# A down projection's last product, divided once more into seven products of 256 columns

## The chip, the cores and the metric

The kernel runs on one core of one Trainium2 chip. The metric is the device time of one execution in microseconds. Before the change it is 525.81 us, the median of three runs (525.75 to 525.83). The core has five engines with a queue each: TensorE (PE in the profile, its weight loads PEld), VectorE (DVE), ScalarE (ACT), GpSimd (POOL) and SyncE (SP), which here issues the DMA transfers. Each engine works through its own queue in order, and semaphores order the queues against each other.

## The reference

```python
# x [1, 2048, 1024], w_gate and w_up [1024, 3584], w_down [3584, 1024], all bfloat16
g = jnp.einsum("bsd,df->bsf", x, w_gate)
u = jnp.einsum("bsd,df->bsf", x, w_up)
h = gelu_tanh(g) * u
return jnp.einsum("bsf,fd->bsd", h, w_down)
```

It is a gated feed-forward layer: two projections up, a product of one with the gelu of the other, and one projection down.

## The kernel before

The 2048 tokens are worked on as four groups of 512. Two groups at a time form a pass, and each pass has a down projection of its own: `down(0, ...)` for the first 1024 tokens and `down(1, ...)` for the rest, one after the other, at the end of the kernel. The change touches these two calls only. What comes before them, the projections up and the gelu, fills the first 346 us of the profile and writes h to DRAM (`hd`), from where it is loaded again in tiles `h[kh][c]`: `kh` is the half of the 3584 features (14 blocks of 128 each, `NJ = 14`), `c` is the group of 512 tokens.

**Seven products instead of eight.** A down projection is a product of 2x2 blocks: token groups by feature halves, times feature halves by output halves (512 columns each). It is made with seven block products and sums before and after them (the Strassen-Winograd form). A block product runs over 14 feature blocks, and for each of these over four banks of 128 tokens, so it has 56 matmuls of 128x128 weights by 512 columns. Four PSUM banks `e` and four banks `c` take the results. In order:

1. `e = h[0][0] * b11` in bf16, copied to `c`; then `c += h[1][0] * b21` in bf16, stored.
2. `e += s2 * t2` (copied out as `u2`), and three blocks behind it `c = s1 * t1` (copied out as `p5`).
3. `e += s3 * t3`, stored with `p5` added, and three blocks behind it `c += s4 * b22`, stored with `u2` added.
4. The last product, `e += h[1][1] * t4`, stored from `e` by ScalarE.

The sums `s1` to `s4` are of h and are made by VectorE (`make12`, `make73`), with results in fp32r, the 32-bit form that TensorE takes at one pass. `t1`, `t2` and `t4` are sums of w_down; they were made in earlier passes and lie in DRAM (`td`), from where `load12` and `load4` fetch them. `t3` is made by VectorE, and `b22` and h[1][1] are cast to fp32r by ScalarE (`tb`, `sa`).

**The second projection's last product is divided.** `down(1)` doesn't run step 4 as 56 matmuls of 512 columns. `inner_product` treats it as a 2x2 product again: 256 tokens (`r` counts its two groups of 128), 7 feature blocks (`H = 7`), 256 columns (`Q = 256`). It has seven products of 2 x 7 = 14 matmuls of 256 columns, 98 in all. `inner_sums` makes its sums s1 to s4 of h[1][1] on VectorE as four instructions of 1792 elements, two at step 20 and two at step 44. `inner_t`, `inner_t3` and `inner_t4` make t1 to t4 of the loaded t4 tiles (`q4`) on POOL, 28 differences of 128x256 elements. `inner_cast` casts the blocks of h[1][1] that are used as they are. z1, z6, z7 and z5 go to the four banks `c`, the other three products are added onto `e`, and VectorE adds both when it stores (`put`). `down(0)` doesn't do this: its step 4 is the plain one.

**What sets the order.** Every engine's order is written out by hand (`tc.manual_schedule`). A projection counts steps: `step(n)` is called before each chunk of 4 or 8 matmuls, from -1 to 75, and runs what `agenda` and `tails` hold for that step (`at`, `at_tail`), then `more(n)`, which for the first projection issues loads for the second. Steps 0 to 13 are the first half of product 1, 14 to 27 its second half, 28 to 44 stage 2, 45 to 61 stage 3, 62 to 75 the last product. ScalarE is ordered by the framework.

**Slots.** Most tiles come from one pool of 58 slots of 2 KB per partition (`slot`). A new tile takes the slot that comes free, and its first writer, a DMA or an engine, waits for the last readers of the tile that had it. DMA transfers all go out of SP's queue, eight semaphore lanes in turn: a transfer that isn't due yet holds up all those behind it.

**The turn from one projection to the next.** The loads of h for `down(1)` are issued by `more_0` in `down(0)`: h[0][0] at step 56, h[1][0] at 59, h[0][1] at 61 and h[1][1] at 63, the last one after the casts of step 4. The second projection's banks `e` are the first one's banks `c` and the other way round. With `SEAM = 3` the first projection holds its first three chunks back, and the first two banks of four chunks are then written before the other two; the second projection doesn't hold them at its start.

Of the kernel before, what the change touches and what calls it, by code (L numbers as in the profile page):

```python
# [10 lines left out]
def kernel(  # L11
# [29 lines left out]
    NJ = NFB // 2  # L41
    N = 512
# [9 lines left out]
    H, Q, R2 = NJ // 2, N // 2, range(2)  # L52
    SLOTS = 58
    STAGED = 3
    SEAM = 3
    LAG = 3
    BIG12 = (0,), (8, 10)
    AT12 = [0, 0, 1, 2, 4, 5, 9, 12, 16, 18, 22, 27, 29, 31], [4, 4, 8, 8, 12, 12, 15, 16, 18, 20, 22, 27, 29, 31]
    AT12S = [6, 7, 9, 10, 13, 14, 16, 18, 20, 23, 25, 27, 29, 31]
    EARLY = 8  # L60
    AT73 = [31 + 2 * j if j < 7 else 38 + j for j in range(NJ)]

    ctx.enter_context(tc.manual_schedule(engines=ORDER))
    xpool = ctx.enter_context(tc.tile_pool(name="x", bufs=1))
    hpool = ctx.enter_context(tc.tile_pool(name="h", bufs=1))
    wpool = ctx.enter_context(tc.tile_pool(name="w", bufs=2))
# [12 lines left out]
    def slot(shape, dtype, name):  # L79
        return kpool.tile(shape, dtype, name=name, tag="k")  # L80
# [18 lines left out]
    def new_h(kh, c):  # L99
        h[kh][c] = hpool.tile([P, NJ, N], bf16, name=f"h{kh}{c}")  # L100
# [4 lines left out]
    def dve(out, a, b, op):  # L105
        nc.vector.tensor_tensor(out=out, in0=a, in1=b, op=op)  # L106
# [4 lines left out]
    def new(eng, a, b, op, name, shape=None, dtype=None):  # L111
        t = slot(shape or [P, N], dtype or f32r, name)
        eng(t, a, b, op)
        return t

    def cast(src, name, shape=None):
        t = slot(shape or [P, N], f32r, name)
        nc.scalar.copy(out=t, in_=src)  # L118
        return t
# [386 lines left out]
    q12, s12, q73, q4, raw = {}, {}, {}, {}, {}  # L506
# [38 lines left out]
        tb = cast(rr[:, 1, :], "tb")  # L545
        q73[j] = s3, t3, s4, tb

    def make_sa(j):
        sa[j] = cast(h[1][1][:, j, :], "sa")

    def fetch12(n):
        kh, j = n // 7, 2 * (n % 7)
        if (1, n) in raw:
# [10 lines left out]
            raw[1, n] = big[:, n - n0]  # L564
            nc.sync.dma_start(out=raw[1, n], in_=wdn[:, kh, j : j + 2, :N])

    def inner_sums(late):
        hi = h[1][1][:, :H], h[1][1][:, H:]
        a11, a21 = hi[0][:, :, :Q], hi[0][:, :, Q:]
        a12, a22 = hi[1][:, :, :Q], hi[1][:, :, Q:]  # L570
        if not late:
            s1, s2 = [xpool.tile([P, H, Q], f32r, name=f"xT{n}") for n in range(2)]
            dve(s1, a21, a22, ADD)
            dve(s2, s1, a11, SUB)
            return s1, s2
        s3, s4 = [wpool.tile([P, H, Q], f32r, name="w") for _ in range(2)]
        dve(s3, a11, a21, SUB)
        dve(s4, a12, inner[1], SUB)
        return s3, s4

    def inner_t(t):
        b1, b2 = q4[t], q4[H + t]
# [27 lines left out]
    for j in range(NJ):  # L610
        at(AT12S[j], make12, j)
        at(AT73[j] - 4, fetch73, j)
        at(AT73[j], make73, j)
    sa, it, inner = {}, {}, []
    tails = {}, {}

    def at_tail(last, step, what, j):
        tails[last].setdefault(int(step), []).append((what, j))
# [3 lines left out]
    for j in range(NJ):  # L622
        for last in range(2):
            if last or j not in STAY:
                at_tail(last, AT12[last][j], lambda j, last=last: load12(j, BIG12[last]), j)
        at_tail(0, 49 + 0.65 * j, load4, j)
        at_tail(0, 54 + 0.55 * j, make_sa, j)
    for t in range(H):
        for j in (t, H + t):
            at_tail(1, 47 + 1.3 * t, load4, j)  # L630
        at_tail(1, 50 + 1.3 * t, inner_t, t)
        at_tail(1, 59, inner_t3, t)
        at_tail(1, 60, inner_t4, t)
        at_tail(1, 53 + 1.1 * t, inner_cast, t)

    def load_h(p, kh, c, j0, j1):
        nc.sync.dma_start(out=h[kh][c][:, j0:j1], in_=hd[p, kh, c][:, j0:j1])

    def todo(step, last):
        for what, j in agenda.get(step, []) + tails[last].get(step, []):  # L640
            what(j)

    def store(ip, c, i, dc, put):
        st = slot([P, N], bf16, "st")
        put(st)
        r0 = (2 * ip + c) * N + i * P
        nc.sync.dma_start(out=out2[r0 : r0 + P, dc * N : (dc + 1) * N], in_=st)

    def inner_product(ip, e, c, ss):
        zz = [hpool.tile([P, 2, N], f32, name=f"h{n}0") for n in range(2)]  # L650
        z1, z6, z7, z5 = [b.rearrange("p (r q) -> p r q", r=2) for b in c]
        T = range(H)
        a11 = [sa[t] for t in T]
        a12 = [sa[H + t][:, :Q] for t in T]
        a22 = [sa[H + t][:, Q:] for t in T]
        b11, b21 = [[q4[h + t][:, :Q] for t in T] for h in (0, H)]
        b22 = [q4[H + t][:, Q:] for t in T]
        t1, t2, t3, t4 = [[it[t][n] for t in T] for n in range(4)]
        s1, s2, s3, s4 = [[s[:, t] for t in T] for s in ss]

        def go(out, lhs, rhs, fresh=False, rs=R2):
            for r in rs:
                for t in T:
                    matmul(
                        out(r), lhs[t][:, r * P : (r + 1) * P], rhs[t],
                        fresh and r == 0 and t == 0, t == H - 1,
                    )

        left, right = slice(0, Q), slice(Q, N)

        def put(i, cols=slice(0, N)):
            r0 = (2 * ip + 1) * N + i * P
            st = slot([P, N], bf16, "st")
            dve(st[:, cols], e[i][:, cols], zz[i // 2][:, i % 2, cols], ADD)
            nc.sync.dma_start(out=out2[r0 : r0 + P, cols], in_=st[:, cols])

        go(lambda r: e[r][:, right], s4, b22, rs=range(1))
        go(lambda r: z1[:, r], a11, b11, True)
        nc.scalar.copy(out=zz[0][:, :, left], in_=z1)
        go(lambda r: z6[:, r], s2, t2, True)  # L680
        u2 = new(dve, z6, zz[0][:, :, left], ADD, "sum", [P, 2, Q], f32)
        go(lambda r: z7[:, r], s3, t3, True)
        dve(zz[1][:, :, left], z7, u2, ADD)
        go(lambda r: z5[:, r], s1, t1, True)
        dve(zz[0][:, :, right], z5, u2, ADD)
        go(lambda r: e[r][:, right], s4, b22, rs=range(1, 2))
        go(lambda r: e[r][:, left], a12, b21, rs=range(1))
        dve(zz[1][:, :, right], z5, zz[1][:, :, left], ADD)
        put(2, right)
        put(3, right)  # L690
        put(0)
        go(lambda r: e[r][:, left], a12, b21, rs=range(1, 2))
        put(1)
        for r in R2:
            go(lambda r: e[2 + r][:, left], a22, t4, rs=range(r, r + 1))
            put(2 + r, left)

    def down(ip, e, c, last, more):
        I = range(NS)

        def step(n):
            todo(n, last)
            if last and n in (20, 44):
                inner.extend(inner_sums(n == 44))
            more(n)

        def chunk(kh, j):
# [12 lines left out]
        for j in range(NJ):  # L720
            step(j)
            held.append((j, chunk(0, j)))
            if j < NJ - SEAM and (last or j >= SEAM):
                for some in (I[:2], I[2:]):
                    for k, rhs in held:
                        rows(e, h[0][0][:, k, :], rhs, k == 0, False, some)
                held = []
# [41 lines left out]
        for i in I:  # L769
            store(ip, 0, i, 1, lambda st: dve(st, c[i], u2[i], ADD))  # L770

        def put21(i):
            store(ip, 1, i, 0, lambda st: nc.scalar.copy(out=st, in_=e[i]))

        if last:
            for j in range(NJ):
                step(4 * NJ + 2 * LAG + j)
            inner_product(ip, e, c, inner)
        else:
            for j in range(NJ):  # L780
                step(4 * NJ + 2 * LAG + j)
                rows(e, sa[j], q4[j], False, j == NJ - 1)
            for i in I:
                put21(i)


    warm = nc.const_aps.tensor(1.0, [P, N], bf16)
# [369 lines left out]
    def more_0(step):  # L1157
        if step == 0:
            load_h(0, 0, 1, 8, NJ)
            load_h(0, 1, 1, 8, NJ - 1)  # L1160
        if step == 32:
            store_made(NJ - 1)
        if step in (56, 59, 61):
            kh, c = {56: (0, 0), 59: (1, 0), 61: (0, 1)}[step]
            new_h(kh, c)
            for j0, j1 in ((0, 4), (4, 8), (8, NJ)):
                load_h(1, kh, c, j0, j1)
        if step == 46:
            fetch_early(0), fetch_early(4)
        if step == 63:  # L1170
            new_h(1, 1)
            for j0, j1 in ((0, 4), (4, 8), (8, NJ)):
                load_h(1, 1, 1, j0, j1)

    E = [E[0][1], E[0][0], E[1][0], E[1][1]]
    down(0, E, F[0] + F[1], False, more_0)
    down(1, F[0] + F[1], E, True, lambda step: None)

# [1 line left out]
_INS = ['x', 'w_gate', 'w_up', 'w_down']  # L1180
# [26 lines left out]
```

## Time and profile before

| what | value |
|---|---|
| median of three runs | 525.81 us |
| the profiled execution | 525.91 us |
| its span in the profile | 524.1 us |
| TensorE busy, granted clock | 519.8 us (99%), 1.0 of full speed |
| VectorE, ScalarE, POOL busy | 396.7, 292.4, 335.4 us |
| first projection's last product | 421.63 to 434.33 us |
| second projection's last product | 509.31 us to the end of TensorE's work at 521.12 us |

In a timeline row the first number is the start in microseconds from the start of the span, the second the length of the group, then engine, line, operation, what is written and read, the shape, and the count; in brackets stands the idle time ahead of it and what ended it. In a group's row the number behind the count is the busy time, then the mean duration in nanoseconds of one. Matmuls are pipelined, so the duration of one is longer than the distance to the next. In a tile's row the three numbers are the shortest, the median and the longest duration in nanoseconds. The line L127 is the matmul helper, L106 VectorE's two-operand sum and L109 POOL's, so that groups are told apart by their tiles.

### The profile page before, as it was taken

The numbers are of one execution on the slowest core, as the hardware profiler recorded it, in microseconds if no ns is written. First come the engines' busy times: TensorE is split into PE (matmuls) and PEld (weight loads), VectorE is DVE, ScalarE is ACT, GpSimd is POOL, SyncE is SP. The second block draws the span as 40 slices with busy tenths as digits, with TensorE's granted clock in tenths as the row PEclk, the third lists the DMA queues.
The fourth block names the chain that finished last, engine by engine and source line by source line (L and its number), as shares of the span: only waits on it lengthen the run. The fifth ranks groups of instructions, "written<-read, shape, count | busy, mean of one in ns | idle before, by whom it ended". The sixth has DMA issues, their size and how long they took to land.

```text
span 524.1 us, 7920 instructions
## 1 busy us (share of the span) xinstructions
PE 519.8 (99%) x2387; PEld 368.7 (70%) x2387; DVE 396.7 (76%) x605; ACT 292.4 (56%) x546; POOL 335.4 (64%) x338
## 2 busy tenths in 40 slices
PE   8999999999999999999999999999999999999997
PEld 5576877767667676767677676754788884488887
DVE  2984558688888989897988989897789326966934
ACT  2546655667778687867777687841135602133430
POOL 1169999999999999999999999740000000000594
PEclk9999999999999999999999999999999999999999
DMA  9961323042625457372827444999987999993742
GB/s 248 220 158 48 96 86 111 22 120 86 197 81 181 124 179 231 110 244 79 275 77 231 162 160 146 354 363 413 386 262 237 394 375 382 392 310 100 238 133 71
DMA packets 102731, 105.91 MB, mean 202 GB/s; under 512 B 19361, under 2 KB 80801, under 8 KB 102689
## 3 DMA queue, kind: packets, MB, share of 16 engines
q1 hardware_dynamic: 102688, 105.41, 61.4%
q8 instruction: 19, 0.31, 0.2%
q14 instruction: 24, 0.19, 0.1%
HBM read 72.61 MB, written 29.62 MB: 195 GB/s over the span
## 4 chain that ended last, share of the span: by engine, by line
PE 98%; DMA 1%; SPq 0%; DVE 0%; issue 0%
PE bank L127 98%; DMA xn<-in_x_dram 1%; SPq L796 0%; PE bank L803 0%; DVE st L106 0%
## 5 line engine op out<-in xcount | busy, mean ns | idle before, releaser
L127 PE MATMUL bank<-h,s 128*128 128x512 f32 x496 | 132.9, 394 | 0.0
L109 POOL TENSOR_TENSOR q<-q 128x256 fp32r<-128x256 f32 x28 | 26.5, 975 | 143.9 <-DMA q<-td 143.3
L127 PEld LDWEIGHTS bank<-h,s 128*128 128x128 f32 x496 | 93.1, 188 | 20.7
L127 PE MATMUL bank<-xT,w 128*128 128x512 bf16 (+1 forms) x472 | 107.0, 376 | 0.0
L127 PEld LDWEIGHTS <-w 128*128 128x128 bf16 x504 | 46.2, 98 | 58.8 <-issue 8.6
L109 POOL TENSOR_TENSOR s<-w 128x512 fp32r<-128x512 bf16 (+1 forms) x76 | 77.7, 1038 | 10.9 <-DMA w<-in_w_gate_dram 10.9
L127 PE MATMUL bank<-t,s 128*128 128x512 f32 x272 | 75.4, 399 | 0.0
L127 PE MATMUL bank<-q 128*128 128x512 f32 x264 | 65.6, 390 | 0.0
L127 PEld LDWEIGHTS bank<-t,s 128*128 128x128 f32 x272 | 51.1, 188 | 11.9
L123 ACT COPY p<-bank 128x512 f32<-128x512 f32 x72 | 40.6, 590 | 29.4 <-PE bank L127 29.4
L127 PEld LDWEIGHTS bank<-q 128*128 128x128 f32 x264 | 49.6, 188 | 10.4
L106 DVE TENSOR_TENSOR q<-h,h 128x512 fp32r<-128x512 bf16 x56 | 38.4, 686 | 16.2 <-DMA h<-hd 16.2
L109 POOL TENSOR_TENSOR s<-s,s 128x256 fp32r<-128x256 f32 x63 | 49.1, 802 | 1.6
L123 ACT COPY u<-bank 128x512 f32<-128x512 f32 x62 | 35.9, 590 | 21.3 <-PE bank L127 21.2
L106 DVE TENSOR_TENSOR xz<-bank,xz 128x512 f32<-128x512 f32 x44 | 30.3, 691 | 19.3 <-PE bank L127 16.9
L127 PEld LDWEIGHTS <-h 128*128 128x128 bf16 x224 | 21.8, 98 | 26.4 <-DMA out_dram<-st 0.3
L109 POOL TENSOR_TENSOR s<-w,s 128x512 fp32r<-128x512 bf16 (+1 forms) x37 | 39.0, 1070 | 0.0
L109 POOL TENSOR_TENSOR s<-s,w 128x512 fp32r<-128x512 f32 (+1 forms) x37 | 37.3, 1023 | 0.9
L118 ACT CAST tb<-raw 128x512 fp32r<-128x512 bf16 x28 | 16.9, 632 | 36.6 <-DMA raw<-in_w_down_dram 26.7
L109 POOL TENSOR_TENSOR m<-raw,m 128x512 fp32r<-128x512 bf16 x28 | 33.8, 1208 | 2.2
L106 DVE TENSOR_TENSOR bank<-bank,u 128x512 f32<-128x512 f32 x49 | 33.7, 689 | 0.0
L106 DVE TENSOR_TENSOR v<-bank,v 128x512 f32<-128x512 f32 x44 | 29.1, 684 | 0.4
(123 smaller groups left out, 918.1 us busy)
## 6 DMA issues: line engine op xcount, KB each, us to landing
raw<-in_w_down_dram SPq DMA_DIRECT2D x68, 256.0 KB, 4.1
q<-td SPq DMA_DIRECT2D x66, 256.0 KB, 5.3
td<-m SPq DMA_DIRECT2D x42, 256.0 KB, 2.8
hd<-o SPq DMA_DIRECT2D x80, 128.0 KB, 1.7
h<-hd SPq DMA_DIRECT2D x17, 512.0 KB, 6.9
hd<-h SPq DMA_DIRECT2D x30, 128.0 KB, 1.7
h<-hd SPq DMA_DIRECT2D x5, 768.0 KB, 7.8
out_dram<-st SPq DMA_DIRECT2D x30, 128.0 KB, 4.0
```

Of the source, the lines that this page charges most:

```text
L106: nc.vector.tensor_tensor(out=out, in0=a, in1=b, op=op)
L109: nc.gpsimd.tensor_tensor(out=out, in0=a, in1=b, op=op)
L118: nc.scalar.copy(out=t, in_=src)
L123: nc.scalar.copy(out=t, in_=ps)
L127: nc.tensor.matmul(ps, lhsT=lhs, rhs=rhs, start=start, stop=stop, skip_group_check=True)
```

## The change

The first projection's last product is divided in the same way as the second's.

- TensorE: the 56 matmuls of 512 columns go. `inner_product` issues 84 of 256 columns at their place, in the order a12 b21 (first half), z1, z6, z5, s4 b22, z7, a12 b21 (second half). The remaining 14, a22 t4, come back as a function `rest`, which the second projection calls at its step 5 (`REST`), after five of its chunks, with the stores of those banks.
- VectorE: `inner_sums` becomes `inner_sum(n)`, one sum a call. In the first projection s1 and s2 are made at step 31, s4 at step 52, s3 behind z6. s3 and s4 go into the tile that held h[1][0]. The z sums go into slots. Two sums of 256 columns for each of the four stores take the place of ScalarE's four copies. In the second projection the sums stay at steps 20 and 44.
- POOL and ScalarE: `inner_t`, `inner_t3`, `inner_t4` and `inner_cast` now run at the same steps of both projections; the 14 casts `make_sa` go.
- Loads: the 14 loads of t4 are issued in pairs (t, 7 + t) at steps 47 to 54 in place of one by one at steps 49 to 57. `load_late` loads h[1][1] behind s3 and h[1][0] behind z7; the loads at steps 59 and 63 go.
- The second projection also holds its first three chunks back at its start.

```diff
+    REST = 5
...
-    def inner_sums(late):
+    def inner_sum(n, place=None):
         hi = h[1][1][:, :H], h[1][1][:, H:]
         a11, a21 = hi[0][:, :, :Q], hi[0][:, :, Q:]
         a12, a22 = hi[1][:, :, :Q], hi[1][:, :, Q:]
...
+        if n < 2:
+            place = xpool.tile([P, H, Q], f32r, name=f"xT{n}")
+        elif place is None:
+            place = wpool.tile([P, H, Q], f32r, name="w")
+        a, b, op = ((a21, a22, ADD), (inner[0], a11, SUB), (a11, a21, SUB), (a12, inner[1], SUB))[n]
+        dve(place, a, b, op)
+        inner[n] = place
...
-        at_tail(0, 49 + 0.65 * j, load4, j)
-        at_tail(0, 54 + 0.55 * j, make_sa, j)
     for t in range(H):
-        for j in (t, H + t):
-            at_tail(1, 47 + 1.3 * t, load4, j)
-        at_tail(1, 50 + 1.3 * t, inner_t, t)
-        at_tail(1, 59, inner_t3, t)
-        at_tail(1, 60, inner_t4, t)
-        at_tail(1, 53 + 1.1 * t, inner_cast, t)
+        for last in range(2):
+            for j in (t, H + t):
+                at_tail(last, 47 + 1.3 * t, load4, j)
+            at_tail(last, 50 + 1.3 * t, inner_t, t)
+            at_tail(last, 59, inner_t3, t)
+            at_tail(last, 60, inner_t4, t)
+            at_tail(last, 53 + 1.1 * t, inner_cast, t)
...
+    def load_late(c):
+        new_h(1, c)
+        for j0, j1 in ((0, 4), (4, 8), (8, NJ)):
+            load_h(1, 1, c, j0, j1)
...
+        if not ip:
+            go(lambda r: e[r][:, left], a12, b21, rs=range(1))
+            go(lambda r: z1[:, r], a11, b11, True)
+            nc.scalar.copy(out=zz[0][0], in_=z1)
+            go(lambda r: z6[:, r], s2, t2, True)
+            inner_sum(2, inner[4][:, 1])
+            load_late(1)
+            u2 = new(dve, z6, zz[0][0], ADD, "sum", [P, 2, Q], f32)
+            go(lambda r: z5[:, r], s1, t1, True)
+            dve(zz[0][1], z5, u2, ADD)
+            go(lambda r: e[r][:, right], s4, b22)
+            go(lambda r: z7[:, r], s3, t3, True)
+            load_late(0)
+            go(lambda r: e[r][:, left], a12, b21, rs=range(1, 2))
+            dve(zz[1][0], z7, u2, ADD)
+            dve(zz[1][1], z5, zz[1][0], ADD)
+            put(0)
+            put(1)
+
+            def rest():
+                for r in R2:
+                    go(lambda r: e[2 + r][:, left], a22, t4, rs=range(r, r + 1))
+                    put(2 + r)
+
+            return rest
...
         def step(n):
+            if n == 31 and not last:
+                inner_sum(0), inner_sum(1)
             todo(n, last)
+            if n == 52 and not last:
+                inner.append(hpool.tile([P, 2, H, Q], f32r, name="h10"))
+                inner_sum(3, inner[4][:, 0])
             if last and n in (20, 44):
-                inner.extend(inner_sums(n == 44))
+                inner_sum(n // 22), inner_sum(n // 22 + 1)
             more(n)
...
-            if j < NJ - SEAM and (last or j >= SEAM):
+            if SEAM <= j < NJ - SEAM:
...
-        if last:
-            for j in range(NJ):
-                step(4 * NJ + 2 * LAG + j)
-            inner_product(ip, e, c, inner)
-        else:
-            for j in range(NJ):
-                step(4 * NJ + 2 * LAG + j)
-                rows(e, sa[j], q4[j], False, j == NJ - 1)
-            for i in I:
-                put21(i)
+        for j in range(NJ):
+            step(4 * NJ + 2 * LAG + j)
+        return inner_product(ip, e, c)
...
-        if step in (56, 59, 61):
-            kh, c = {56: (0, 0), 59: (1, 0), 61: (0, 1)}[step]
+        if step in (56, 61):
+            kh, c = {56: (0, 0), 61: (0, 1)}[step]
...
-        if step == 63:
-            new_h(1, 1)
-            for j0, j1 in ((0, 4), (4, 8), (8, NJ)):
-                load_h(1, 1, 1, j0, j1)
...
-    down(0, E, F[0] + F[1], False, more_0)
-    down(1, F[0] + F[1], E, True, lambda step: None)
+    rest = down(0, E, F[0] + F[1], False, more_0)
+
+    def more_1(step):
+        if step == REST:
+            rest()
+
+    down(1, F[0] + F[1], E, True, more_1)
```

More of the change, by code (lines that the diff above doesn't have):

```diff
@@ L546, in make73 @@
         q73[j] = s3, t3, s4, tb
-    def make_sa(j):
-        sa[j] = cast(h[1][1][:, j, :], "sa")
     def fetch12(n):
@@ L570, in inner_sums @@
         a12, a22 = hi[1][:, :, :Q], hi[1][:, :, Q:]
[L571 to L579, printed above, removed]
+        if n < 2:
[5 more added lines that the diff above has]
+        inner[n] = place
     def inner_t(t):
@@ L613 @@
         at(AT73[j], make73, j)
-    sa, it, inner = {}, {}, []
+    sa, it, inner = {}, {}, [None] * 4
     tails = {}, {}
@@ L647, in store, with inner_product @@
         nc.sync.dma_start(out=out2[r0 : r0 + P, dc * N : (dc + 1) * N], in_=st)
-    def inner_product(ip, e, c, ss):
-        zz = [hpool.tile([P, 2, N], f32, name=f"h{n}0") for n in range(2)]
+    def inner_product(ip, e, c):
+        z = [hpool.tile([P, 2, N], f32, name=f"h{n}0") for n in range(2)] if ip else None
+        zz = [
+            [z[m][:, :, n * Q : (n + 1) * Q] if ip else slot([P, 2, Q], f32, "z") for n in R2]
+            for m in R2
+        ]
         z1, z6, z7, z5 = [b.rearrange("p (r q) -> p r q", r=2) for b in c]
@@ L658, in inner_product @@
         t1, t2, t3, t4 = [[it[t][n] for t in T] for n in range(4)]
-        s1, s2, s3, s4 = [[s[:, t] for t in T] for s in ss]
+        s1, s2, s3, s4 = range(4)
         def go(out, lhs, rhs, fresh=False, rs=R2):
+            if isinstance(lhs, int):
+                lhs = [inner[lhs][:, t] for t in T]
             for r in rs:
@@ L673, in put @@
             st = slot([P, N], bf16, "st")
-            dve(st[:, cols], e[i][:, cols], zz[i // 2][:, i % 2, cols], ADD)
-            nc.sync.dma_start(out=out2[r0 : r0 + P, cols], in_=st[:, cols])
+            if ip:
+                dve(st[:, cols], e[i][:, cols], z[i // 2][:, i % 2, cols], ADD)
+            else:
+                for n, side in enumerate((left, right)):
+                    dve(st[:, side], e[i][:, side], zz[i // 2][n][:, i % 2], ADD)
+            nc.sync.dma_start(out=out2[r0 : r0 + P, cols], in_=st[:, cols])
@@ L677, in inner_product @@
         go(lambda r: e[r][:, right], s4, b22, rs=range(1))
         go(lambda r: z1[:, r], a11, b11, True)
-        nc.scalar.copy(out=zz[0][:, :, left], in_=z1)
+        nc.scalar.copy(out=zz[0][0], in_=z1)
         go(lambda r: z6[:, r], s2, t2, True)
-        u2 = new(dve, z6, zz[0][:, :, left], ADD, "sum", [P, 2, Q], f32)
+        u2 = new(dve, z6, zz[0][0], ADD, "sum", [P, 2, Q], f32)
         go(lambda r: z7[:, r], s3, t3, True)
-        dve(zz[1][:, :, left], z7, u2, ADD)
+        dve(zz[1][0], z7, u2, ADD)
@@ L684, in inner_product @@
         go(lambda r: z5[:, r], s1, t1, True)
-        dve(zz[0][:, :, right], z5, u2, ADD)
+        dve(zz[0][1], z5, u2, ADD)
         go(lambda r: e[r][:, right], s4, b22, rs=range(1, 2))
         go(lambda r: e[r][:, left], a12, b21, rs=range(1))
-        dve(zz[1][:, :, right], z5, zz[1][:, :, left], ADD)
+        dve(zz[1][1], z5, zz[1][0], ADD)
         put(2, right)
@@ L770, in down @@
             store(ip, 0, i, 1, lambda st: dve(st, c[i], u2[i], ADD))
-        def put21(i):
-            store(ip, 1, i, 0, lambda st: nc.scalar.copy(out=st, in_=e[i]))
-        if last:
-            for j in range(NJ):
-                step(4 * NJ + 2 * LAG + j)
-            inner_product(ip, e, c, inner)
-        else:
-            for j in range(NJ):
-                step(4 * NJ + 2 * LAG + j)
-                rows(e, sa[j], q4[j], False, j == NJ - 1)
-            for i in I:
-                put21(i)
+        for j in range(NJ):
+            step(4 * NJ + 2 * LAG + j)
+        return inner_product(ip, e, c)
     warm = nc.const_aps.tensor(1.0, [P, N], bf16)
```

## The prediction

> **What bounds the kernel.** I read the page's busy times first, then the chain that ended last, then TensorE's timeline around the edit, then the queues beside it.
>
> ```profile
> span 524.1 us, 7920 instructions
> PE 519.8 (99%) x2387; PEld 368.7 (70%) x2387; DVE 396.7 (76%) x605; ACT 292.4 (56%) x546; POOL 335.4 (64%) x338
> PE 98%; DMA 1%; SPq 0%; DVE 0%; issue 0%
> 7.65 513.48 PE bank L127 x2344
> ```
>
> The fourth line, from the chain in order of time, says that from 7.65 us on the chain never leaves TensorE. So a change is worth what it takes out of TensorE's stream, less any wait it puts into it. The stretches of that stream (start, length, group, count):
>
> ```profile
> 421.63 12.86 PE L127 MATMUL bank<-q,sa 128*128 128x512 f32 x56
> 434.33 13.99 PE L127 MATMUL bank<-w,h 128*128 128x512 bf16 x64
> 509.31 1.00 PE L127 MATMUL bank<-q,w 128*128 128x256 f32 x7
> 517.60 3.52 PE L127 MATMUL bank<-q,sa 128*128 128x256 f32 x28
> L127 PE MATMUL bank<-q,sa 128*128 128x256 f32 x42 | 5.4, 283 | 0.0
> L127 PEld LDWEIGHTS bank<-q,sa 128*128 128x128 f32 x98 | 15.7, 190 | 2.2
> ```
>
> The first is the product that the edit replaces: 434.33 - 421.63 = 12.70 us for 56 matmuls, 226.8 ns each, no gap. The next two show the divided form, which the second projection already runs: 70 of its matmuls start between 509.31 and 517.60, so 8.29 / 70 = 118.4 ns each; the last 28 take (3.52 - 0.28) / 27 = 120 ns. A single 256-column matmul shows 283 ns and its weight load 190 ns, but these overlap; the start-to-start distance is the price.
>
> **The change, part by part.**
>
> *TensorE.* Removed: 56 x 226.8 = 12.70 us. Added: 98 matmuls of 256 columns (84 in place, 14 for T4 after five of the next projection's chunks, 20 matmuls). At 118.4 ns they take 11.60 us, with the last 28 at 120 ns 11.65 us. Gain 1.05 to 1.10; I take 1.07. Going between the f32 and bf16 streams: by 434.33 the bf16 group starts exactly 56 distances after 421.63, and 434.33 to 509.31 (74.98 us) is 112 x 216 ns (13.99 less a last one of 0.38, over 63) plus 224 x 226.8 ns = 74.99. So a switch costs below 0.05 us; T4 adds two. The new order at the start of the second projection (three chunks held) moves matmuls and adds none.
>
> [...]
>
> *VectorE.* Added: four 1792-element sums, one 512-element sum and three z sums, eight half-row stores' sums.
>
> ```profile
> 377.15 0.68 DVE L106 TENSOR_TENSOR q<-h,h 128x512 fp32r<-128x512 bf16 x1
> 382.31 0.69 DVE L106 TENSOR_TENSOR q<-raw 128x512 fp32r<-128x512 bf16 x1 [4.47 <-DMA raw<-in_w_down_dram]
> 409.19 0.68 DVE L106 TENSOR_TENSOR q<-h,q 128x512 fp32r<-128x512 bf16 x1
> 417.52 2.48 DVE L106 TENSOR_TENSOR st<-bank,p 128x512 bf16<-128x512 f32 x4 [7.65 <-PE bank L127]
> 421.15 2.48 DVE L106 TENSOR_TENSOR st<-bank,u 128x512 bf16<-128x512 f32 x4 [1.14 <-PE bank L127]
> 436.38 0.69 DVE L106 TENSOR_TENSOR q<-h,h 128x512 fp32r<-128x512 bf16 x1 [12.74 <-DMA h<-hd]
> 448.41 2.02 DVE L106 TENSOR_TENSOR xT<-h 128x1792 fp32r<-128x1792 bf16 x1
> 450.47 2.02 DVE L106 TENSOR_TENSOR xT<-xT,h 128x1792 fp32r<-128x1792 f32 x1
> 462.52 0.69 DVE L106 TENSOR_TENSOR q<-raw 128x512 fp32r<-128x512 bf16 x1 [3.87 <-DMA raw<-in_w_down_dram]
> ```
>
> s1 and s2 (2.02 us each, the rows of 448.41) go in at 377.15, ahead of the sum there; they end about 381.2 and that sum at 381.9, before 382.31, when the raw data that VectorE waited 4.47 us for arrive. Cost nothing. s4 goes behind 409.19, 409.9 to 411.9, inside 7.65 us idle. s3 goes behind the four sums of 421.15: 423.6 to 425.7; its user z7 starts 63 matmuls in, at 421.63 + 63 x 0.1184 = 429.1, so it may be 3.4 us late. The z sums follow TensorE; the one that gates TensorE is the last (it frees z5's bank): z7 ends at 421.63 + 77 x 0.1184 = 430.8, two sums of 0.69 end by 432.3, and the bank is first written after 84 x 0.1184 + 8 x 0.216 us, at 433.3: 1.0 us spare. Then VectorE waits for T4 (ends 421.63 + 9.95 + 20 x 0.216 + 1.66 = 437.6) and stores it by about 438.6, so the second projection's sums begin 2.2 us later than 436.38. Behind them the wait of 3.87 us before 462.52 takes that up.
>
> *POOL.* Added: 28 differences of 128x256; POOL is otherwise idle there. The second projection has the same 28:
>
> ```profile
> 490.23 7.35 POOL L109 TENSOR_TENSOR q<-q 128x256 fp32r<-128x256 f32 x1 [143.32 <-DMA q<-td]
> 490.23 27.02 POOL L109 TENSOR_TENSOR q<-q 128x256 fp32r<-128x256 f32 x28 [143.32 <-DMA q<-td]
> L109 POOL TENSOR_TENSOR q<-q x28: 732/738/7352, 490.2 to 516.5; 128x256 fp32r<-128x256 f32 x28
> 496.30 0.69 DVE L106 TENSOR_TENSOR q<-h,q 128x512 fp32r<-128x512 bf16 x1
> L106 DVE TENSOR_TENSOR o<-v,v x20: 685/916/1605, 107.9 to 327.7; 128x512 bf16<-128x512 f32 x20
> ```
>
> The first took 7352 ns: it ended 0.6 us after VectorE's unbroken run of SBUF-to-SBUF sums (last start 496.30). The other 27 take (27.02 - 7.35) / 27 = 0.73 us each, also while VectorE adds from PSUM. So in the first projection:
>
> ```profile
> 403.08 9.11 SPq L530 DMA_DIRECT2D q<-td  x13
> DMA to landing us min/median/max: 4.7/5.3/7.8
> ```
>
> SP reaches the T4 loads at the same place, 403.08; the first lands at 407.8 to 410.9. VectorE's run ends with s4 at 411.9. I let the first difference end at 412.6, the k-th 0.73 (k-1) later, and s3 take POOL's turn for 2.0 us. t2 (14th) at 422.1, needed from 424.1; t3 (21st) at 412.6 + 14.6 + 2.0 = 429.2, needed at 421.63 + 69 x 0.1184 = 429.8; t4 (28th) at 434.3, needed at 436.6. The tight one is t3, with 0.6 us. Its bounds: if s4 doesn't hold POOL, up to 2 us earlier; if each big sum costs one more POOL turn of 0.73, up to 0.9 us late. I take 0, nearest the row of 738 ns. The loads themselves are issued later now (TensorE must free their slots): the last waits for a matmul that stands 45 ahead of the product, so it goes at about 421.63 - 45 x 0.2268 + 0.4 = 411.8 and lands by 419.6 (7.8), for a difference that starts at 420.6.
>
> *SP and the loads.* The T4 loads are paired and the third h load (h10) now waits for z7, the fourth (h11) for s3; stores and weight loads queue behind them.
>
> ```profile
> 412.54 1.65 SPq L637 DMA_DIRECT2D h<-hd  x3
> 429.45 2.79 SPq L637 DMA_DIRECT2D h<-hd  x3
> 436.43 3.98 SPq L556 DMA_DIRECT2D raw<-in_w_down_dram  x5
> DMA to landing us min/median/max: 5.8/7.3/10.4
> 421.63:434.33 12.70, 12.70 (x58) 10.33 (x56) 2.01 (x4) 0.48 (x2) 0.00 (x0) 1.00 1.04 376
> ```
>
> h11 goes at about 426, before the old last load at 429.45, and VectorE wants it at 438.6. h10 goes at 430.9 to 433 and lands by 443.4 at the longest (10.4); TensorE wants it at 431.6 + 56 x 0.216 + 1.66 = 445.3. The five raw loads follow the first two stores, at about 434.5 to 438.5, not later than 436.43 to 440.4. The DMA engines are full there (the last row is a stretch by windows; 1.04 is their share, 376 the GB/s), so bytes only change places. Cost nothing, with 1.9 us in hand for h10.
>
> *ScalarE.* Three casts fewer, one copy more, and the four output copies of this row gone; it waits for TensorE, so nothing on the path.
>
> ```profile
> 433.85 2.05 ACT L773 CAST st<-bank 128x512 bf16<-128x512 f32 x4 [17.37 <-PE bank L127]
> ```
>
> *Sum.* 12.70 - 11.63 = 1.07 us less. The profiled execution took 525.91 us, so 524.84; the runs' median is 0.10 below it: 525.81 - 1.07 = 524.74. The bound of 0.2% (about what a measurement can tell from no change) is 1.05 us, so the forecast sits on that bound; every unforeseen wait pushes it to the "no change" side. I forecast 524.8.
>
> **The rivals.**
>
> *t3 or t4 late.* POOL's chain slips by its bound of 0.9 us past t3's 0.6 spare, or by a bit more through a late T4 load (7.8 against 5.3): TensorE stops 0.3 to 1.0 us in z7 or T4. Time 525.0 to 525.8. For it: spare of 0.6 us only; against: 27 of 28 differences at 738 ns.
>
> *s3 starves (slower).* s3 reads SBUF twice while POOL runs without a pause. If POOL kept VectorE out as VectorE kept POOL out for 7.35 us, s3 would start when POOL runs dry, 412.6 + 27 x 0.73 = 432.3, and end at 434.3; z7 would stop until then, 5.2 us: 524.74 + 5.2 = 529.9. It loses from a delay of 3.4 + 1.07 = 4.5 us on. Against it: the o<-v,v sums also read SBUF twice beside a busy POOL and took 1605 ns at most, 0.92 over the shortest. [...]
>
> *h10 late.* If landing took more than 12.3 us, TensorE would wait in the second half of the projection's first product; 16 us would cost 3.7: 527.4. Against: the longest seen is 10.4.
>
> *No gain.* If weight loads bound at 190 ns, 98 would take 18.6 us: 531.7. The 118.4 ns of the same form speak against it.
>
> **How the numbers follow.** The forecast (gain 0.85 to 1.15, 524.65 to 524.95) 0.62, of which 0.38 lies beyond the 0.2%; t3 or t4 late 0.23, of which 0.02 slower; s3 starved 0.08; h10 late 0.04; no gain or another wait 0.03. Faster 0.38; same 0.24 + 0.21 + 0.02 = 0.47; slower 0.02 + 0.08 + 0.04 + 0.01 = 0.15. The range runs from 524.6 to 525.7: the forecast and nearly all of the late-POOL case.
>
> **What would show it.** TensorE: 84 matmuls of 256 columns in about 9.95 us from 421.6, 14 more about 435.9, no idle row at either; the bf16 stream at 431.6. POOL: 28 differences from about 409 to 434, the last of t3 before 429.8. VectorE: s3 not longer than 2.8 us. An idle row on TensorE released by POOL or VectorE between 429 and 437, or by a load of h near 445, would prove it wrong.

## The result, and the profile after

The changed kernel takes 524.84 us (median of 17 runs, 524.28 to 525.28) against 525.75 us for the kernel before (17 runs, 524.89 to 526.31): a ratio of 0.9984, 95% interval 0.9977 to 0.9992. That is 0.9 us less, and the interval doesn't reach 1; the size lies inside the 0.2% that the prediction set as the bound of "faster". The profiled execution shown here took 525.15 us, span 523.4 us.

From the page of the changed kernel (span, busy times, shares of the chain):

```profile
span 523.4 us, 8060 instructions
PE 518.3 (99%) x2429; PEld 369.8 (71%) x2429; DVE 411.0 (79%) x621; ACT 289.8 (55%) x540; POOL 359.1 (69%) x366
PE 98%; DMA 1%; SPq 0%; DVE 0%; issue 0%
```

From its chain of work in order of time:

```profile
7.90 512.48 PE bank L128 x2386
```

The bound hasn't changed: 42 more matmuls (2429 against 2387) in 1.5 us less busy time, and the chain still stays on TensorE to the end. It now gets there at 7.90 us, where before it was 7.65 us: this execution lost a quarter of a microsecond at the start, in work that the change doesn't touch. Runs of one kernel lie 1.0 us apart after the change and 1.4 us before it (524.89 to 526.31), more than the whole difference. So I compare kernels below by a *stretch* that leaves the start out: from the start of the first projection's last product to the start of the second's. It holds all that the change adds and moves up to there. Before: 509.31 - 421.63 = 87.68 us, from the rows in the prediction.

TensorE's timeline of the changed kernel:

```profile
421.89 2.67 PE L128 MATMUL bank<-q,sa 128*128 128x256 f32 x21
424.40 3.44 PE L128 MATMUL bank<-q,xT 128*128 128x256 f32 x28
427.67 3.52 PE L128 MATMUL bank<-q,h 128*128 128x256 f32 x28
431.03 1.00 PE L128 MATMUL bank<-q,sa 128*128 128x256 f32 x7
431.87 4.49 PE L128 MATMUL bank<-w,h 128*128 128x512 bf16 x20
436.01 2.02 PE L128 MATMUL bank<-q,sa 128*128 128x256 f32 x14
437.87 9.67 PE L128 MATMUL bank<-w,h 128*128 128x512 bf16 x44
508.56 1.00 PE L128 MATMUL bank<-q,w 128*128 128x256 f32 x7
```

The new stretch is 508.56 - 421.89 = 86.67 us, so the change is worth 1.01 us on TensorE. The 84 matmuls (the first four rows) take 431.87 - 421.89 = 9.98 us; 20 bf16 chunks follow, and then the 14 of T4. No row has a bracket: the profile names no idle time of TensorE here.

VectorE's timeline of the changed kernel: s1 and s2, the wait that they went into, the last sum of raw data, s4, s3, and the first sum of the second projection:

```profile
377.07 2.02 DVE L107 TENSOR_TENSOR xT<-h 128x1792 fp32r<-128x1792 bf16 x1
379.12 2.02 DVE L107 TENSOR_TENSOR xT<-xT,h 128x1792 fp32r<-128x1792 f32 x1
382.17 0.69 DVE L107 TENSOR_TENSOR q<-raw 128x512 fp32r<-128x512 bf16 x1 [0.43 <-PE bank L128]
408.31 0.69 DVE L107 TENSOR_TENSOR q<-raw 128x512 fp32r<-128x512 bf16 x1 [1.19 <-DMA raw<-in_w_down_dram]
409.64 2.44 DVE L107 TENSOR_TENSOR h<-h,xT 128x1792 fp32r<-128x1792 bf16 x1
423.81 2.61 DVE L107 TENSOR_TENSOR h<-h 128x1792 fp32r<-128x1792 bf16 x1
438.79 0.68 DVE L107 TENSOR_TENSOR q<-h,h 128x512 fp32r<-128x512 bf16 x1
```

The 4.47 us of waiting ahead of the raw sum have become 4.04 us of work and 0.43 us of waiting. s4 and s3 (the rows of 409.64 and 423.81) take 2.44 and 2.61 us instead of 2.02. That fits a wait for the difference that POOL had in hand: the extra 0.42 and 0.59 us are less than one difference, 0.73.

POOL's timeline of the changed kernel. The first row is the whole group; the others are parts of it, seen through short windows (the 2nd difference, the 14th, the 19th, the 21st and 22nd, the 28th):

```profile
409.00 24.25 POOL L110 TENSOR_TENSOR q<-q 128x256 fp32r<-128x256 f32 x28 [62.28 <-DVE q L107]
410.28 2.40 POOL L110 TENSOR_TENSOR q<-q 128x256 fp32r<-128x256 f32 x1
421.01 0.73 POOL L110 TENSOR_TENSOR q<-q 128x256 fp32r<-128x256 f32 x1
424.49 2.52 POOL L110 TENSOR_TENSOR q<-q 128x256 fp32r<-128x256 f32 x1
427.67 1.43 POOL L110 TENSOR_TENSOR q<-q 128x256 fp32r<-128x256 f32 x2
432.53 0.72 POOL L110 TENSOR_TENSOR q<-q 128x256 fp32r<-128x256 f32 x1
```

The first difference got in at 409.00, ahead of s4 at 409.64; s4 then held the second (2.40 us), and s3 held the 19th (2.52 us). What the first one waited for was VectorE: the bracket names it, and 409.00 is where VectorE's last sum of raw data ends (408.31 + 0.69). That sum had itself waited for its load. In every kernel below that starts from the changed one, the first difference also starts within 0.04 us of that sum's end (in the run with four repeats the bracket names TensorE, at the same moment). So POOL's start, which lies between 408.67 and 410.44 us, moves with the landing of one load. t2 was complete with the 14th, at 421.7, and is wanted by the seventh matmul of z6 at 424.40 + 6 x 0.118 = 425.1: 3.4 us in hand. t3 was complete with the 21st, at 428.40, and is wanted at 427.67 + 20 x 0.118 = 430.04: 1.64 in hand. t4 was complete at 433.25, wanted at 436.01 + 6 x 0.118 = 436.72: 3.47 in hand.

SyncE's queue in the changed kernel (start, time of issuing, line, transfer, count):

```profile
403.35 9.60 SPq L531 DMA_DIRECT2D q<-td  x14
426.48 6.01 SPq L632 DMA_DIRECT2D h<-hd  x6
434.38 3.75 SPq L554 DMA_DIRECT2D raw<-in_w_down_dram  x5
```

The two late loads, h11 (h[1][1]) and h10 (h[1][0]), go out as six transfers from 426.48 to 432.49, and the raw loads follow at 434.38.

### The profile page after: what moved, and what is told of

Its sections match the earlier page's. It is cut to its first block, busy times and chain, and to the rows that moved or that the text cites. A ratio compares the mean times of both kernels' runs of the same rounds, so it can differ in the third digit from the quotient of the medians.

```text
span 523.4 us, 8060 instructions
## 1 busy us (share of the span) xinstructions
PE 518.3 (99%) x2429; PEld 369.8 (71%) x2429; DVE 411.0 (79%) x621; ACT 289.8 (55%) x540; POOL 359.1 (69%) x366
## 4 chain that ended last, share of the span: by engine, by line
PE 98%; DMA 1%; SPq 0%; DVE 0%; issue 0%
PE bank L128 98%; DMA w<-in_w_up_dram 1%; SPq L827 0%; SPq L847 0%; DVE st L107 0%
## 5 line engine op out<-in xcount | busy, mean ns | idle before, releaser
L110 POOL TENSOR_TENSOR q<-q 128x256 fp32r<-128x256 f32 x56 | 50.4, 928 | 119.4 <-DVE q L107 62.3
L128 PEld LDWEIGHTS bank<-q 128*128 128x128 f32 x264 | 49.6, 188 | 10.4
```

The lines of the kernel that those rows point to most:

```text
L110: nc.gpsimd.tensor_tensor(out=out, in0=a, in1=b, op=op)
L128: nc.tensor.matmul(ps, lhsT=lhs, rhs=rhs, start=start, stop=stop, skip_group_check=True)
```

## The experiments

Each run is one profiled execution, read by its stretch. What an experiment costs is its stretch less 86.67 us (the changed kernel's), or less 87.68 us where it starts from the kernel before.

### The narrow matmuls alone

In the kernel before, each matmul of the last product is issued as two of 256 columns; nothing else changes.

```diff
-                rows(e, sa[j], q4[j], False, j == NJ - 1)
+                for side in (slice(0, Q), slice(Q, N)):
+                    rows([b[:, side] for b in e], sa[j], q4[j][:, side], False, j == NJ - 1)
```

> The kernel before, with the 56 matmuls of 512 columns of the first projection's last product run as 112 matmuls of 256 columns (same operands, no division). Measure: the stretch from the start of that product to the start of the second projection's last product, 87.68 us before and 86.67 us after the change. Theory (a matmul costs its start-to-start distance, 118.4 ns at 256 columns and 226.8 ns at 512): 112 x 0.1184 = 13.26 in place of 12.70, so the stretch is 88.24 us, 0.56 longer. Rival (weight loads of 190 ns bound in a long run of narrow matmuls): 112 x 0.19 = 21.3, stretch 96.3. Rival (two halves cost as much as one whole): 87.68.

TensorE's timeline of this kernel:

```profile
421.79 13.59 PE L127 MATMUL bank<-q,sa 128*128 128x256 f32 x112
435.22 10.97 PE L127 MATMUL bank<-w,h 128*128 128x512 bf16 x50
510.21 1.00 PE L127 MATMUL bank<-q,w 128*128 128x256 f32 x7
```

The stretch is 510.21 - 421.79 = 88.42 us, 0.74 more. One narrow matmul takes (435.22 - 421.79) / 112 = 119.9 ns, so the weight loads (188 to 190 ns by their own rows) do not bound it. This splits the gain in two: 112 narrow matmuls cost 0.73 us more than 56 wide ones (0.56 was expected, at 118.4 ns), and the division then drops 14 of the 112, 14 x 119.9 ns = 1.68 us. The difference is 0.95 us, which accounts for nearly all of the 1.01.

### T4 at its own place

The changed kernel with `rest()` called as soon as the first projection has returned, and not at step 5 of the second.

```diff
     rest = down(0, E, F[0] + F[1], False, more_0)
+    rest()
...
         if step == REST:
-            rest()
+            pass
```

> The changed kernel with the 14 T4 matmuls at the end of the first projection in place of step 5 of the second. In the profile of the change the last seven differences of POOL (t4) end between 429.1 and 433.25 us, and TensorE would want the first at 431.87 and the seventh at 432.6. Theory (the deferral covers POOL's chain): TensorE stops about 0.65 us in T4, the stretch is 87.3 us in place of 86.67. Rival (the deferral covers nothing, POOL is early enough): 86.67.

TensorE's timeline of this kernel:

```profile
421.50 2.67 PE L128 MATMUL bank<-q,sa 128*128 128x256 f32 x21
432.67 0.38 PE L128 MATMUL bank<-q,sa 128*128 128x256 f32 x1 [0.30 <-POOL q L110]
433.35 1.21 PE L128 MATMUL bank<-q,sa 128*128 128x256 f32 x8 [0.30 <-POOL q L110]
509.40 1.00 PE L128 MATMUL bank<-q,w 128*128 128x256 f32 x7
```

The stretch is 87.90 us: 1.23 more than the changed kernel, and 0.22 more than the kernel before. TensorE now waits for POOL's last differences of t4, twice. POOL ends at 433.29, as in the changed kernel, while TensorE would want the last one at 421.50 + 90 x 0.1185 = 432.16, 1.13 us earlier. So without the move of T4 there is no gain. (It came out larger than expected, 0.65 us, mainly because this execution reached the product 0.39 us earlier while POOL kept its time.)

### The order at the second projection's start

The changed kernel with the condition of before: the second projection doesn't hold its first three chunks back.

```diff
-            if SEAM <= j < NJ - SEAM:
+            if j < NJ - SEAM and (last or j >= SEAM):
```

> The changed kernel without the three held chunks at the start of the second projection (each chunk writes all four banks from the first on). In the profile of the change VectorE frees the bank of z5 at 432.64 us; without the held chunks TensorE wants that bank three matmuls in, at 431.87 + 3 x 0.216 = 432.5, and the bank of z7 (freed at 431.92) at 432.3. Theory: TensorE stops 0.1 to 0.3 us, the stretch is 86.8 to 87.0. Rival (the order of the chunks itself wins or costs something): a difference with no idle time on TensorE at 432.

TensorE's timeline of this kernel around T4; then the fourth and fifth of the 20 bf16 matmuls alone, seen through the window from 432.24 to 432.50 us; then VectorE's sum that frees the bank of z5:

```profile
431.40 4.66 PE L128 MATMUL bank<-w,h 128*128 128x512 bf16 x20
435.71 2.02 PE L128 MATMUL bank<-q,sa 128*128 128x256 f32 x14
432.23 0.59 PE L128 MATMUL bank<-w,h 128*128 128x512 bf16 x2
431.49 0.69 DVE L107 TENSOR_TENSOR z<-bank,z 128x512 f32<-128x512 f32 x1
```

The stretch is 508.26 - 421.42 = 86.84 us, 0.17 more, and it sits in the first 20 bf16 matmuls: 435.71 - 431.40 = 4.31 us instead of 4.14. In the changed kernel and the seven others below these 20 take 4.13 to 4.14 us, so 0.17 is clear of their scatter. It falls where the expectation put it. The fourth matmul is the first to write the bank of z5. It would start at 431.40 + 3 x 0.216 = 432.05 and starts at 432.23, 0.05 us after VectorE's sum has read that bank (431.49 + 0.69 = 432.18). So the new order is worth 0.17 us, by keeping TensorE off a bank that isn't free yet; the profile gives so short a stop no bracket.

### POOL made late ahead of t2 and t3

The changed kernel with its first difference of t1 repeated two, three and four times. In the kernel with three, the 2 is a 3, and in the one with four a 4. (The run with four came first; the other two expectations draw on it.)

```diff
     def inner_t(t):
...
+        for _ in range(2 if t == 0 and len(inner) == 4 else 0):
+            pool(ta[:, 0], b1[:, Q:], b1[:, :Q], SUB)
```

Two more:

> The changed kernel with POOL's first difference of the first projection made three times (two more; in the run with four more each cost 0.8 us, so 1.6 us later in all). Measured as before: the stretch from the first projection's last product to the second's, 86.67 us after the change. Theory (t3 has 1.65 us spare by the ends of POOL's operations, t2 2.7 us as long as it ends before VectorE's s3 takes POOL's turn): no stop or one below 0.1 us, stretch 86.7. By the spare of 0.6 us that the prediction worked out: a stop of 1.0 us in z7, stretch 87.7.

Three more:

> As the run with two more differences, with three more (2.4 us). t2's last difference would now end at 424.8, one microsecond behind the time at which VectorE asks for s3. Theory A (whichever waits first gets the turn): s3 goes ahead of t2's last difference, which ends about 426.5 in place of 425.1 where TensorE wants it: a stop of 1.4 to 2.0 us in z6, as in the run with four more. Theory B (POOL's queue keeps its turn): t2 is in time and only t3 is late, a stop of 0.7 us in z7, stretch 87.4. Whether the granted clock falls behind a stop of this length, as it did behind the 1.99 us of the run with four more (0.5 from 428 to 431 us), is open; if it does, about as much again is lost.

Four more:

> The changed kernel with POOL's first difference of the first projection made five times in place of once (four more of 0.70 us, 2.8 us in all, no other work). In the profile of the change the last t3 ends at 428.4 and TensorE wants it at 429.33 + 0.71 = 430.0; the last t4 ends at 433.25 and is wanted at 436.8. Theory (t3 is the tight one, with 1.65 us spare): TensorE stops 2.8 - 1.65 = 1.15 us in z7, stretch 87.8. By the spare of 0.6 us that the prediction worked out: 2.2 us, stretch 88.9. Rival (POOL has more slack than the ends of its operations show): 86.67.

Timelines of the kernel with two more, TensorE's and then POOL's:

```profile
421.35 2.67 PE L128 MATMUL bank<-q,sa 128*128 128x256 f32 x21
423.86 0.87 PE L128 MATMUL bank<-q,xT 128*128 128x256 f32 x6
426.51 2.84 PE L128 MATMUL bank<-q,xT 128*128 128x256 f32 x22 [1.77 <-POOL q L110]
```

```profile
410.44 25.72 POOL L110 TENSOR_TENSOR q<-q 128x256 fp32r<-128x256 f32 x30 [62.99 <-DVE q L107]
424.07 2.38 POOL L110 TENSOR_TENSOR q<-q 128x256 fp32r<-128x256 f32 x1
```

The stop is at the seventh matmul of z6, for t2, and not in z7 for t3, where it was expected. t2's last difference (here the 16th) is the row of 424.07: s3, which VectorE began at 423.27, went ahead of it, and the difference took 2.38 us with that wait. The stretch is 510.06 - 421.35 = 88.71 us, 2.04 more. With three more it is 510.01 - 421.50 = 88.51 us, 1.84 more, and the same stop:

```profile
426.47 2.83 PE L128 MATMUL bank<-q,xT 128*128 128x256 f32 x22 [1.59 <-POOL q L110]
```

Counted at the place itself, the seventh matmul of z6 would have started at 423.86 + 6 x 0.118 = 424.57 us and started at 426.51: 1.94 of the 2.04 us. With three more it would have started at 424.01 + 0.71 = 424.72 and started at 426.47: 1.75 of the 1.84. Three more cost no more than two, because POOL started 0.87 us earlier in that run (409.57 against 410.44 us): in both, s3 came up just ahead of t2's last difference. t3 came in time behind this stop.

With four more the same matmul would have started at 423.75 + 0.71 = 424.46 us and started at 426.61, 2.15 us late. But the stretch is 511.71 - 421.24 = 90.47 us, 3.80 more. TensorE's timeline of this kernel, and then a view by windows (behind the window's length the busy time and count of PE, PEld, DVE, ACT and POOL; the last three columns are the granted clock, the share of the DMA engines and GB/s):

```profile
426.61 4.12 PE L128 MATMUL bank<-q,xT 128*128 128x256 f32 x22 [1.99 <-POOL q L110]
```

```profile
427.60:428.00 0.40, 0.40 (x5) 0.40 (x5) 0.07 (x1) 0.00 (x0) 0.40 (x2) 0.74 1.05 376
428.00:431.00 3.00, 3.00 (x16) 3.00 (x16) 0.85 (x2) 0.00 (x0) 3.00 (x5) 0.50 1.07 415
431.00:431.40 0.40, 0.40 (x4) 0.40 (x4) 0.40 (x1) 0.00 (x0) 0.40 (x2) 0.75 0.98 394
```

Behind the stop the granted clock fell to 0.50. The means of the two 0.40 us slices, 0.74 and 0.75, put the fall at 427.79 and the return at 431.20 us: 3.41 us at half speed, which cost 1.71 us. With the 2.15 us of the stop that makes 3.86, against 3.80 measured. The windows of the kernels with two and three more show a clock of 1.00 throughout.

### POOL made late ahead of t4

The same with the last difference of t4, in the first projection only: six and nine repeats (a 9 in place of the 6).

```diff
     def inner_t4(t):
+        for _ in range(6 if t == H - 1 and inner[2] is None else 0):
+            pool(it[t][3], q4[H + t][:, :Q], it[t][1], SUB)
         pool(it[t][3], q4[H + t][:, :Q], it[t][1], SUB)
```

Six more:

> The changed kernel with POOL's last difference of t4 delayed by six more differences of the same size (0.8 us each, the price of an extra one in the run with four: 4.8 us). t4 had about 3.65 us in hand, so TensorE should stop for about 1.15 us inside T4, at one place. Theory A (behind a stop of about 2 us or longer the granted clock can fall to half for 3.5 us, and a shorter one costs only itself): the clock stays at 1.0, and the stretch from the first projection's last product to the second's is 86.67 + 1.15 = 87.8 us. Theory B (any stop ahead of a product makes it fall): about 1.7 us more, 89.5.

Nine more:

> The same with nine differences (7.2 us): TensorE should stop for about 3.55 us inside T4. Theory A: the granted clock falls to about half for some 3.5 us behind the stop, and the stretch is 86.67 + 3.55 + 1.7 = 91.9 us. Theory B gives the same here. Theory C (the half clock behind the 1.99 us stop in the run with four differences had nothing to do with the stop): the clock stays at 1.0 and the stretch is 90.2.

TensorE's timeline with six more, and then with nine more:

```profile
438.57 1.22 PE L128 MATMUL bank<-q,sa 128*128 128x256 f32 x8 [1.90 <-POOL q L110]
```

```profile
441.11 2.07 PE L128 MATMUL bank<-q,sa 128*128 128x256 f32 x8 [4.31 <-POOL q L110]
```

Six more: the stretch is 510.32 - 421.48 = 88.84 us, 2.17 more, at a clock of 1.00. POOL ended at 438.52, so t4 was late by 5.27 + 0.41 - 3.47 = 2.21 us: the stop costs itself and nothing else. It was longer than the expected 1.15 us because POOL started 0.43 us later and TensorE 0.41 us earlier than in the changed kernel, and t4 had 3.47 us in hand where 3.65 was taken. Theory B (any stop makes the clock fall) is out.

Nine more: the stretch is 515.79 - 421.61 = 94.18 us, 7.51 more. POOL ended at 441.05, t4 late by 7.80 + 0.28 - 3.47 = 4.61 us. The other 2.9 us are the clock's, as the windows of this kernel show:

```profile
436.80:440.00 3.20, 0.00 (x0) 0.00 (x0) 0.00 (x0) 0.00 (x0) 2.89 (x5) 1.00 1.04 378
440.00:441.00 1.00, 0.00 (x0) 0.00 (x0) 0.00 (x0) 0.00 (x0) 0.92 (x2) 0.73 1.10 371
441.00:447.00 6.00, 5.89 (x18) 3.32 (x19) 4.41 (x9) 0.00 (x0) 0.05 (x1) 0.50 0.99 307
447.00:447.50 0.50, 0.50 (x4) 0.12 (x2) 0.40 (x2) 0.00 (x0) 0.00 (x0) 0.72 0.81 211
```

It fell at 440.46, still inside the stop, and came back at 447.28 us: 6.82 us, twice the 3.41 of the other run. TensorE worked for 6.17 us of that, which half speed would price at 3.1 us at most, near the 2.9 that are left. Theory C is out. The length of a stop alone does not decide whether the drop comes: it followed the stop of 1.99 us, while behind stops of 1.59, 1.77, 1.90 and 2.19 us (the last below) the clock stayed at 1.00. No run here shifts a stop of the same length, so what decides between stops of about 2 us stays open.

### h10 loaded later

The changed kernel with `load_late(0)` moved from behind z7 to the end of `rest`, behind T4's stores.

```diff
             go(lambda r: z7[:, r], s3, t3, True)
-            load_late(0)
...
                     put(2 + r)
+                load_late(0)
```

> The changed kernel with the load of h[1][0] behind the T4 part in place of behind z7. In the profile of the change its three transfers are issued from about 430.9 to 432.5 and TensorE wants the first third at 445.6. Here they stand behind the T4 stores, which SP issues at 442.2 to 443.3; with 5.8 us to landing the first third comes at about 449.5. Theory (the load had about 7 us in hand and is then a plain wait): TensorE stops 3.5 to 5 us at the second half of the first product, and if the granted clock falls behind a stop of this length, up to 2 us more: stretch 90.2 to 93.7. Rival (transfers in front of it give way, as the bytes are the same): below 1 us.

TensorE's timeline of this kernel, and then its SyncE queue:

```profile
447.05 1.90 PE L128 MATMUL bank<-w,h 128*128 128x512 bf16 x8 [2.19 <-DMA h<-hd]
```

```profile
440.60 2.85 SPq L632 DMA_DIRECT2D h<-hd  x3
```

The stretch is 509.95 - 420.93 = 89.02 us, 2.35 more. That is less than expected, because SyncE got to the load sooner than I had put it. TensorE asks for h10 behind the first 36 matmuls of the group that follows T4: in the changed kernel at 437.87 + 36 x 0.216 = 445.65 us. There the last piece is issued by 432.49, and the six late pieces land like this:

```profile
DMA to landing us min/median/max: 5.3/6.3/7.8
```

At the longest, 7.8 us, it is in by 440.3: 5.4 us in hand.

### VectorE's run broken

The changed kernel with a write of one column by VectorE, which reads nothing, behind each `make73` of the second projection, that is behind every third sum.

```diff
+        if len(inner) == 5:
+            nc.vector.memset(tick, 0.0)
...
+    tick = xpool.tile([P, 1], f32, name="tick")
```

> The changed kernel with one small VectorE instruction (a memset of one column, no SBUF input) behind each three sums of the second projection's third stage. In the profile of the change POOL's first difference of the second projection took 7587 ns, to the end of VectorE's run of sums that read SBUF twice. [...] Theory B (POOL is only let in when VectorE idles): 7 us or more again. [...]

POOL's 28 differences in the second projection (shortest, median, longest in ns), in the changed kernel and then in this one:

```profile
L110 POOL TENSOR_TENSOR q<-q x28: 728/738/7587, 489.2 to 515.7; 128x256 fp32r<-128x256 f32 x28
```

```profile
L110 POOL TENSOR_TENSOR q<-q x28: 731/750/1245, 489.1 to 513.7; 128x256 fp32r<-128x256 f32 x28
```

The longest falls from 7587 to 1245 ns and POOL is done 2.0 us sooner. So the long wait comes from VectorE's unbroken run of sums (tiles of h, q and raw, 0.69 us each), and a small write behind every third sum is enough to let POOL in. Theory B (POOL is only let in when VectorE idles) is out: it gave 7 us or more again. POOL doesn't come in at the write itself. It asked at 489.14 us, while VectorE worked on the first sum behind a write (from 488.76), and came in ahead of the next sum (from 489.36), where no write stands; that sum took 1.23 us instead of 0.69. How the write does this stays open, and so does whether another instruction in its place, or a mere pause, would do the same. TensorE gains nothing that one execution could show (stretch 507.76 - 421.19 = 86.57 us, 0.10 less): POOL was in time there anyway.

## Why the prediction was right

**The gain on TensorE.** The working gave 1.07 us (1.05 to 1.10), and the stretch shows 1.01. The three pieces 9.98 + 4.14 + 1.86 us, less 20 bf16 chunks at 0.216, leave 11.66 us for the 98 matmuls, against 11.60 to 11.65. T4 between bf16 chunks looks 0.2 us dearer than 14 x 118.4 ns and the chunks ahead of it 0.2 us cheaper: the two cancel, probably because the streams overlap at the switches, which no run here separates. The distances of the rows held.

**VectorE.** Every place came as forecast: s1 and s2 in the raw wait, s4 behind 409.6, s3 at 423.81, the second projection's sums from 438.79 (438.6). The "s3 starves" rival is out: s3 took 2.61 us, 0.59 more than its 2.02, which is less than one difference, and 2.01 to 2.61 in the other kernels that start from the changed one. The limit of 2.8 us that the prediction set for s3 was an estimate, 2.02 plus one difference of 0.73. POOL's wait in the second projection is of another size: its difference took 7.59 us, in which eleven of VectorE's sums began and ended.

**POOL: right outcome, mis-sized margin.** All 28 differences came in time, but the step "I let the first difference end at 412.6" failed. That step took it that VectorE's sums would shut POOL out up to the end of s4, as they do in the second projection. But the first difference could go as soon as the last sum of raw data was done, got in at 409.00, before s4, and s4 held only the second. A difference costs 0.69 to 0.74 us where 0.73 was taken; t3 has 1.64 us in hand, not 0.6, and t4 3.47, not 2.3. t3 is the operand with the least, as said. What the text missed is how a slip would show: a difference that isn't begun when s3 comes up waits 1.6 us more (2.38 us instead of 0.74), so TensorE stops at t2 before t3 is even asked for.

**The price of that rival was incomplete.** "TensorE stops 0.3 to 1.0 us" counted the wait alone. That is right for the stops that left the clock alone: with two, three and six repeats the stretch grew by as much as the operand was late, within 0.1 us. But the stop with four repeats was followed by half a clock for 3.41 us, and then it cost 3.8. The rival stayed away. Had it come as in these runs, at 1.8 us or more, it would have gone past the range's upper end, which lies 0.9 us above the forecast.

**Loads.** The raw loads went out from 434.38 to 438.13 (434.5 to 438.5 forecast), h11 at 426.48 (426). h10 had 5.4 us in hand, not 1.9: it was issued by 432.5, landed in 7.8 us at most where 10.4 was allowed, and TensorE wanted it 0.3 us later. (The time that the working gives for "h10 late", 527.4, is a slip in the sum: 524.74 + 3.7 is 528.4.)

**The move of T4 and the new order** were costed at nothing, rightly: they add no time. But they carry the result: without the move 1.23 us are lost, without the order 0.17.

**The sum.** 524.8 against a median of 524.84. Part of that closeness is luck: the medians lie 0.91 us apart where 1.07 was worked out, the kernel before now has a median of 525.75, and single runs of one kernel scatter by 1.0 to 1.4 us. The range, up to 525.7, would also have held a gain of next to nothing; the stretch is the better witness. The gain sits just inside the bound of 0.2%, as the text said it might.

## What to carry to other kernels

When TensorE has no gaps, price an edit by the distance between starts in a row of the same form; it was good to 0.06 us here, where durations of single matmuls (283 ns for a distance of 118) would have given a loss. For every operand that another engine makes, work out when it is done and when it is wanted, and ask whose turn stands between: this change gains 1 us only because the last operand was given 4.1 us more by moving its product behind 20 other matmuls. And price a possible stop of TensorE of about 2 us or more with the clock drop that may follow it, not by its length alone: here the one of 1.99 us cost 3.80 us, the one of 4.31 us 7.51.

## What the runs showed of the hardware that was not expected

- A stop of TensorE of 1.99 us was followed by 3.41 us at a granted clock of 0.50, with one of 4.31 us it was 0.50 for 6.82 us, from 0.65 us before the end of the stop; stops of 1.59, 1.77, 1.90 and 2.19 us left it at 1.00.
- VectorE's unbroken run of sums stretched a POOL difference to 7.6 us, where the median was 0.74; one small write behind every third sum brought that to 1.2 us. In the other direction POOL's 28 differences in a row, in the first projection, delayed s3 and s4 by no more than 0.59 us.
